# The first down product of a fused attention and two-MLP kernel: blocks of 512 tokens instead of 288

## The chip, the cores and the metric

The kernel runs on one core of one Trainium2 chip. The metric is the device time of one execution in microseconds. Beside it stands the profile of one execution, whose span runs from its first instruction to its last.

## The reference, cut to what matters

Two attentions follow each other (a packed query of 32 rows against 576 keys, then 576 queries against the 32 packed rows), and their output goes through two MLPs over 4608 tokens (8 batches of 576), with 512 features outside and 2048 inside:

```python
x = attention(q, attention(p, k, v))          # 4608 x 512
h = x @ w_in;   x = (h * np.cos(h)) @ w_out   # first MLP, d_ff 2048
h = x @ w_in2
g = np.where(h >= 1, h, np.where(h <= -1, 0.0, (h + 1) ** 2 / 4))
out = g @ w_out2                              # second MLP
```

## The kernel before, in words

All large products run on TensorE in float32r. For accuracy each operand is split into a high part and a remainder, and a product is three matmuls (`TERMS`: high times high, high times low, low times high) that add up in PSUM. Every matmul has a 128x128 stationary operand of its own and moves 288 columns (half a batch of 576 tokens).

The program has four stages, one after the other on TensorE.

- **up1** (L501 `up`): 128 items, each one half batch and one pair of 128-row tiles of d_ff. An item is 12 matmuls into `hps` and one ScalarE copy `u` (L516), which is stored to DRAM as `h1T` (late_store, L517). The attention's work is folded into the first items. The products that form an item's weights (`form`, L336) and the conversion of `w_out` (`cut_w_out`) lie among the items too. `hps` has two buffers, `u` five.
- **down1** (L720 `run_down1`): the product `g @ w_out` of the first MLP. It walks 16 blocks of 288 tokens. A block has 8 iterations, one for each pair of d_ff tiles, and an iteration is 24 matmuls (2 tiles of d_ff, 4 tiles of the output, 3 terms) at L745. So there are 128 iterations and 3072 matmuls. A block adds up in two PSUM tiles: tags X and Y in even blocks, two buffers of Z in odd ones; each tile is two PSUM banks of 512 float32 columns, of which `bank` (L582) hands out 288.
- **up2** (L790 `run_up2`) and **down2** (L909 `run_down2`): the second MLP, with seven products for eight of 2x2 blocks (X1, Z6, Y5 and so on). Its matmuls stand at L607 and L952.

An iteration i of down1 also makes ready what later iterations need. `load_h1(i + 7)` reads 288 tokens of `h1T`. `turn_k` (ScalarE, L691), `turn_t` (VectorE, L696), `turn_s` (ScalarE, a sine, L703) and `turn_m` (VectorE, L708) make h cos h; `part_hi` (ScalarE, L713) and `part_lo` (VectorE, L718) split it into `r`, which the matmuls move. All of these work on 128x576 elements. In the order written at L749 to L754 they run one to four iterations ahead of the matmuls that use them.

Further work in down1: `step("wt")` does one step of `combine` (L423), which converts the second MLP's weights into the forms of the seven products; a unit of weights is 13 steps, and down1 does 8 units, one in each 15 iterations. Each block's result is copied out of PSUM to `o` in the next block (ScalarE for c = 0, L761; VectorE for c = 1, L759) and stored as `yT`. `SU_AT` names the iterations that load converted weights (`load_su`), `Y_LOAD` and the last nine iterations prepare the first batch of up2 (`make_y`).

The order of instructions on each engine is the order in which they are written (`in_order`, L1198). All DMAs are issued from SP's queue, also in written order. A tile that takes over memory of a closed pool waits for the last user of that memory. The last seven items of up1 already carry the preparation of down1's first iterations (`begin`, L1194), and its first seven loads stand at every second of the last 14 items. Pools: `wpool` has eight buffers of 8 KB a partition, and `r`, `g` (the loads) and `t` have pools of their own (L1216 to L1218).

Of the kernel before, what the change touches and what calls it, by code (L numbers as in the profile page):

```python
# [23 lines left out]
SU_AT = tuple(range(70, 94, 4)) + (122, 124, 126, 127)  # L24
Y_LOAD = 112
# [12 lines left out]
def body(ctx: ExitStack, tc: tile.TileContext, q, k, v, p, w_in, w_out, w_in2, w_out2, out):  # L38
# [21 lines left out]
    dram = ctx.enter_context(tc.tile_pool(name="dram", bufs=1, space=bass.MemoryType.DRAM))  # L60

    yT = dram.tile([DM, NT], F32, name="yT")
    h1T = dram.tile([NFT // 2, 128, NT // HB, 2, HB], F32, name="h1T")
    su = dram.tile([2, 7, 128, 2, 2, 512], F32, name="su")
    sd = dram.tile([7, 2, 128, 4, 2, 256], F32, name="sd")
    gT = dram.tile([NFT // 2, 128, NT // HB, 2, HB], F32, name="gT")
# [22 lines left out]
    def late_store(dst, src):  # L89
        stores.append((dst, src))  # L90
# [410 lines left out]
    def up(n, hf, fp):  # L501

        c = fp // 2
        m, x = M[n, c], AT[n, hf]
        hps = ps_h.tile([128, 2, 512], F32, tag="h", name="hps")
        for j in range(2):
            cs = slice((fp % 2 * 2 + j) * 128, (fp % 2 * 2 + j) * 128 + 128)
            for G in range(2):
                for i, (w, y) in enumerate(TERMS):
                    nc.tensor.matmul(  # L510
                        out=hps[:, j, :HB], lhsT=m[:, w, G, cs], rhs=x[:, G, y],
                        start=(G == 0 and i == 0), stop=(G == 1 and i == 2),
                    )
        u = wk.tile([128, 2, HB], F32, tag="u", name="u", bufs=5)
        if True:
            last_act[:] = [nc.scalar.activation(out=u, in_=hps[:, :, :HB], func=AF.Copy).ins]  # L516
        late_store(h1T[fp, :, 2 * n + hf], u)  # L517


    KS = {"X1": 0, "Y5": 3, "X2": 1, "Z6": 4, "Y3": 6, "Z7": 5, "Z4": 2}  # L520
# [2 lines left out]
    n_s = [0]  # L523

    def s_tile(src):
        pool, tag, bufs = ((mpool, "m", 2), (wpool, "w", 8), (mpool, "o", 4))[(0, 0, 1, 1, 1, 1, 1, 1, 1, 1, 2, 2, 2, 2)[n_s[0] % 14]]
# [52 lines left out]
        tile_of("Z4", b21)  # L579
        yield  # L580

    def bank(x):  # L582
        return ps2.tile([128, 2, 512], F32, tag=x, name="ps" + x, bufs=2 if x == "Z" else 1)[:, :, :HB]

    def wtile(pool, tag, bufs):
        return pool.tile([128, 2, HB], F32, tag=tag, name=tag, bufs=bufs)
# [87 lines left out]

    pu, pd = ExitStack(), ExitStack()
    dn1 = {}

    G1 = {}

    def load_h1(i):  # L680
        if i < B * 16:
            t = dn1["g"].tile([128, 2, HB], F32, tag="g", name="h1")
            nc.sync.dma_start(out=t, in_=h1T[i % 8, :, i // 8])
            G1[i] = t

# [13 lines left out]

    def turn_s(i):  # L700
        if i < B * 16:
            t = turns[i]
            nc.scalar.activation(out=t, in_=t, func=AF.Sin, scale=2 * PI, bias=halfpi)  # L703

    def turn_m(i):
        if i < B * 16:
            t = turns[i]
            nc.vector.tensor_tensor(out=t, in0=G1.pop(i), in1=t, op=ALU.mult)  # L708

    def part_hi(i):  # L710
        if i < B * 16:
            r = parts[i] = dn1["r"].tile([128, 2, 2, HB], F32R, tag="r", name="r1")
            nc.scalar.activation(out=r[:, 0], in_=turns[i], func=AF.Copy)  # L713

    def part_lo(i):
        if i < B * 16:
            r = parts[i]
            nc.vector.tensor_tensor(out=r[:, 1], in0=turns.pop(i), in1=r[:, 0].bitcast(F32), op=ALU.subtract)  # L718

    def run_down1(w_out_ops):  # L720
        prep[:] = [ctx.enter_context(tc.tile_pool(name="prep", bufs=1, reuse_waits="tile"))]
        for x in range(5):
            up2[x] = ctx.enter_context(tc.tile_pool(name=f"up_{x}", bufs=1, reuse_waits="tile"))
        po = pd.enter_context(tc.tile_pool(name="dn_o", bufs=3, reuse_waits="tile"))
        streams["wt"].append(combine(units[N_FIRST:], prep_tiles))
        eng = [nc.vector]
        ys = make_y(0, eng)
        n_su = [0]
        order = [(ch, o) for ch in range(2) for o in ORDER_UP]

        for i in range(B * 16):
            blk, c = divmod(i, 8)
            if c == 0:
                acc = early if blk == 1 else [bank("Z") for _ in range(2)] if blk % 2 else [bank(x) for x in "XY"]
# [14 lines left out]
            part_lo(i + 1)  # L749
            turn_m(i + 2)  # L750
            turn_t(i + 3)
            turn_k(i + 4)
            part_hi(i + 2)
            turn_s(i + 3)  # L754
            begin_stores()
            if blk and c < 2:
                y = po.tile([128, 2, HB], F32, tag="o", name="o1")
                if c:
                    nc.vector.tensor_copy(out=y, in_=done[c])  # L759
                else:  # L760
                    nc.scalar.activation(out=y, in_=done[c], func=AF.Copy)  # L761
                late_store(
                    yT[c * 256:c * 256 + 256, (blk - 1) * HB:blk * HB].rearrange("(j p) t -> p j t", p=128), y
                )
# [4 lines left out]
            if i in SU_AT:  # L769
                load_su(*order[n_su[0]])  # L770
                n_su[0] += 1
            if i == Y_LOAD or i >= B * 16 - 9:
                next(ys)
        for c in range(2):
            y = po.tile([128, 2, HB], F32, tag="o", name="o1")
            if c:
                nc.vector.tensor_copy(out=y, in_=done[c])
            else:
                nc.scalar.activation(out=y, in_=done[c], func=AF.Copy)
            late_store(  # L780
                yT[c * 256:c * 256 + 256, NT - HB:].rearrange("(j p) t -> p j t", p=128), y
            )
# [7 lines left out]
    def run_up2():  # L790
# [7 lines left out]
        for p in range(B):  # L798
            for f in range(0, 8, 2):
# [10 lines left out]
                for k, o in enumerate(("X1", "Z4", "Z6", "Y5", "X2", "Z7", "Y3")):  # L810
# [375 lines left out]
    def item():  # L1186
        i = pos[0]
        for x in events[i]:
# [2 lines left out]
        begin_stores(1)  # L1191
        pos[0] += 1

    begin = [[lambda: turn_k(0), lambda: turn_t(0)], [lambda: turn_k(1), lambda: turn_t(1)],  # L1194
             [lambda: turn_s(0), lambda: turn_m(0)], [lambda: turn_k(2), lambda: turn_t(2)],
             [lambda: turn_s(1), lambda: turn_m(1), lambda: turn_k(3)],
             [lambda: part_hi(0), lambda: part_lo(0), lambda: turn_s(2), lambda: part_hi(1)], []]
    in_order = ordered(E.PE, E.Activation, E.DVE, E.SP, E.Pool)  # L1198
    if True:
        start()  # L1200
# [9 lines left out]
        while pos[0] < len(items):  # L1210
            i = pos[0]
            if i == len(items) - 16:
# [6 lines left out]
            if i >= len(items) - 14 and i % 2 == 0:  # L1219
                load_h1((i - len(items) + 14) // 2)  # L1220
            if i >= len(items) - 7:
                for x in begin[i - len(items) + 7]:
                    x()
# [59 lines left out]
```

## Time and profile before

| what | us |
|---|---|
| median of 3 runs (1474.38 to 1475.12) | 1474.67 |
| the profiled execution's own time | 1473.97 |
| its span, first to last instruction | 1472.2 |
| up1 in it, with the start | 0 to 339.1 |
| down1 | 339.1 to 748.7 |
| up2 | 748.7 to 1109 |
| down2 | 1109 to 1472 |

PE is TensorE, PEld its loading of stationary operands, DVE VectorE, ACT ScalarE, POOL GpSimd, SPq the queue from which SP issues DMAs. A line such as L745 is a line of the kernel before. Matmuls overlap in their pipeline: the mean of one (some 296 ns) is the time from its start to its last result, and the pace is read from how many fit into a stretch.

### The profile page before, as it was taken

How to read it: one execution, taken by the hardware profiler on the slowest of the kernel's cores; microseconds unless marked ns; L12 is line 12 of the kernel's file. 1: busy time of each engine (PE TensorE's matmuls, PEld its weight loads, DVE VectorE, ACT ScalarE, POOL GpSimd, SP SyncE). 2: the span in 40 equal slices, each digit the busy share in tenths (PEclk: the TensorE clock that was granted, in tenths of full speed). 3: DMA queues.
4: the chain of work that ended last, by engine and by line, in shares of the span. 5: the costliest groups of instructions: out<-in, count | busy, mean ns of one | idle time of the engine just before them, and what ended most of it. 6: DMA issues, size and time to landing. Idle time of an engine off the chain costs nothing.

```text
span 1472.2 us, 29608 instructions
## 1 busy us (share of the span) xinstructions
PE 1444.5 (98%) x11800; PEld 1390.2 (94%) x11800; DVE 1161.3 (79%) x1653; ACT 905.7 (62%) x1418; POOL 133.4 (9%) x85
## 2 busy tenths in 40 slices
PE   7999999999999999999999999999999999999998
PEld 5777878889999999999999999999999999999998
DVE  7875869778889888988846988889968777777775
ACT  4655666667767676766657777777775444444443
POOL 0000000000000000000005433533400000000000
PEclk9999999999999999999999999999999999999999
DMA  9777896675765567766664364664588544343350
GB/s 344 269 249 250 291 323 220 233 250 176 213 178 156 163 204 233 249 194 212 195 262 165 140 217 173 216 216 163 209 326 329 209 149 154 110 136 126 122 161 33
DMA packets 155961, 302.35 MB, mean 205 GB/s; under 512 B 13488, under 2 KB 59568, under 8 KB 152240
## 3 DMA queue, kind: packets, MB, share of 16 engines
q1 hardware_dynamic: 155824, 300.47, 60.2%
q8 instruction: 92, 1.51, 0.4%
q14 instruction: 45, 0.37, 0.1%
HBM read 176.69 MB, written 123.73 MB: 204 GB/s over the span
## 4 chain that ended last, share of the span: by engine, by line
PE 72%; DVE 2%; issue 1%; DMA 1%; ACT 0%; DVEq 0%; SPq 0%; ACTq 0%
PE psZ L745 14%; PE psZ L952 10%; PE psZ L607 9%; PE psY L745 7%; PE psX L745 7%; PE psX L952 7%; PE psY L952 6%; PE psY L607 6%; PE psX L607 6%; DMA t<-gT 1%; DVE t L627 1%; DVE hh L595 0%; PE hps L510 0%; DVE pa L147 0%; DVE u L595 0%
## 5 line engine op out<-in xcount | busy, mean ns | idle before, releaser
L510 PEld LDWEIGHTS hps<-at,m 128*128 128x128 f32 x1536 | 209.1, 191 | 41.6 <-ACT u L516 21.6
L510 PE MATMUL hps<-at,m 128*128 128x288 f32 x1536 | 222.9, 302 | 8.9 <-ACT u L516 5.5
L745 PE MATMUL psZ<-r,wo 128*128 128x288 f32 x1536 | 206.1, 296 | 0.0
L745 PEld LDWEIGHTS psZ<-r,wo 128*128 128x128 f32 x1536 | 205.2, 188 | 0.0
L855 ACT ACTIVATE r<-g 128x576 fp32r<-128x576 f32 x147 | 97.0, 681 | 123.3 <-DVE g L852 112.1
L77 POOL TENSOR_TENSOR ty<-yb,ty 128x576 fp32r<-128x576 f32 x51 | 85.6, 1678 | 935.0 <-ACT ty L76 934.2
L713 ACT ACTIVATE r<-t 128x576 fp32r<-128x576 f32 x128 | 87.6, 685 | 128.2 <-PE psY L745 61.3
L718 DVE TENSOR_TENSOR r<-t,r 128x576 fp32r<-128x576 f32 x128 | 96.9, 757 | 57.4 <-ACT r L713 57.1
L516 ACT ACTIVATE u<-hps 128x576 f32<-128x576 f32 x128 | 83.1, 649 | 79.5 <-PE hps L510 48.6
L745 PE MATMUL psY<-r,wo 128*128 128x288 f32 x768 | 123.1, 296 | 0.0
L745 PE MATMUL psX<-r,wo 128*128 128x288 f32 x768 | 123.1, 296 | 0.0
L627 DVE SCALAR_TENSOR_TENSOR t<-hh,t 128x576 f32<-128x576 f32 x128 | 122.2, 974 | 0.0
L619 ACT ACTIVATE t<-hh,half 128x576 f32<-128x576 f32 x128 | 98.9, 772 | 34.6 <-DVE hh L595 33.3
L865 DVE TENSOR_TENSOR r<-g,r 128x576 fp32r<-128x576 f32 x147 | 107.6, 753 | 4.7 <-ACT r L855 4.7
L745 PEld LDWEIGHTS psY<-r,wo 128*128 128x128 f32 x768 | 109.4, 188 | 0.0
L745 PEld LDWEIGHTS psX<-r,wo 128*128 128x128 f32 x768 | 109.3, 188 | 0.0
L952 PE MATMUL psZ<-r,so 128*128 128x288 f32 x768 | 104.8, 295 | 0.6 <-DVE hh L988 0.6
L952 PE MATMUL psY<-r,sw 128*128 128x288 f32 x768 | 104.6, 295 | 0.0
L952 PEld LDWEIGHTS psZ<-r,so 128*128 128x128 f32 x768 | 102.9, 188 | 0.8 <-DVE hh L988 0.8
L952 PEld LDWEIGHTS psY<-r,sw 128*128 128x128 f32 x768 | 102.8, 188 | 0.0
L708 DVE TENSOR_TENSOR t<-h,t 128x576 f32<-128x576 f32 x128 | 96.3, 752 | 1.8 <-ACT t L703 1.8
L696 DVE SCALAR_TENSOR_TENSOR t<-h,t 128x576 f32<-128x576 f32 x128 | 96.3, 752 | 1.8 <-ACT t L691 1.8
(170 smaller groups left out, 2625.0 us busy)
## 6 DMA issues: line engine op xcount, KB each, us to landing
h1T<-u SPq DMA_DIRECT2D x128, 288.0 KB, 4.2
h<-h1T SPq DMA_DIRECT2D x128, 288.0 KB, 3.9
gT<-t SPq DMA_DIRECT2D x128, 288.0 KB, 2.9
g<-gT SPq DMA_DIRECT2D x85, 288.0 KB, 3.7
raw<-in_moe_w_out SPq DMA_DIRECT2D x32, 512.0 KB, 6.7
t<-gT SPq DMA_DIRECT2D x36, 288.0 KB, 4.2
k<-in_k SPq DMA_DIRECT2D x8, 1152.0 KB, 9.1
yT<-o SPq DMA_DIRECT2D x32, 288.0 KB, 2.4
```

Source lines behind the costliest of these rows:

```text
L510: nc.tensor.matmul(out=hps[:, j, :HB], lhsT=m[:, w, G, cs], rhs=x[:, G, y], start=(G == 0 and i == 0), stop=(G == 1 and i == 2),)
L607: nc.tensor.matmul(out=ps[:, i], lhsT=s[:, d, w, cs], rhs=t[:, d, y], start=first and d == n == 0, stop=d == 1 and n == 2, skip_group_chec ...
L619: nc.scalar.activation(out=t, in_=st["h", o], func=AF.Relu, scale=0.5, bias=half)
L627: nc.vector.scalar_tensor_tensor(out=t, in0=st["h", o], scalar=1.0, in1=t, op0=ALU.max, op1=ALU.min)
L696: nc.vector.scalar_tensor_tensor(out=t, in0=G1[i], scalar=1 / (2 * PI), in1=t.bitcast(I32), op0=ALU.mult, op1=ALU.subtract)
L708: nc.vector.tensor_tensor(out=t, in0=G1.pop(i), in1=t, op=ALU.mult)
L713: nc.scalar.activation(out=r[:, 0], in_=turns[i], func=AF.Copy)
L718: nc.vector.tensor_tensor(out=r[:, 1], in0=turns.pop(i), in1=r[:, 0].bitcast(F32), op=ALU.subtract)
L745: nc.tensor.matmul(out=acc[d // 2][:, d % 2], lhsT=wo[f // 4, w][:, f % 4, ds], rhs=r[:, y, k], start=f == n == 0, stop=f == NFT - 1 and n ...
L855: nc.scalar.activation(out=r[:, 0], in_=b[out], func=AF.Copy)
L865: nc.vector.tensor_tensor(out=r[:, 1], in0=src, in1=r[:, 0].bitcast(F32), op=ALU.subtract)
L952: nc.tensor.matmul(out=ps[:, j], lhsT=w_[:, (2 * c + k) % 4, w, j * 128:j * 128 + 128], rhs=r[:, y, k], start=first_k and k == n == 0, sto ...
```

## The change

Down1 walks 9 blocks of 512 tokens, so 72 iterations of 24 matmuls with 512 columns each, and every instruction of the preparation covers 128x1024 elements. `h1T` is laid out with the tokens of all blocks side by side, so that a store writes 256 pieces of 288 floats and a load reads 256 pieces of 512. The three `r` tiles are taken from `wpool` and used in turn; the loads have 5 buffers in place of 7, `o` 2 in place of 3. A load stands 6 iterations ahead in place of 7. In an iteration the steps of the weights' conversion move ahead of `turn_t`; a unit's 13 steps now lie in 8 iterations (`STEPS_1`) and the eighth unit ends with iteration 63. The loads of converted weights and the first batch's preparation have new places (`SU_AT`, `Y_STEPS`), the preparation of down1's first iterations begins 12 items before the end of up1 in place of 7, and the first loads 16 items before in place of 14.

```diff
-    h1T = dram.tile([NFT // 2, 128, NT // HB, 2, HB], F32, name="h1T")
+    h1T = dram.tile([NFT // 2, 128, 2, NT], F32, name="h1T")
...
-        late_store(h1T[fp, :, 2 * n + hf], u)
+        t0 = n * S + hf * HB
+        late_store(h1T[fp, :, :, t0:t0 + HB], u)
...
-        pool, tag, bufs = (...)[(0, 0, 1, 1, 1, 1, 1, 1, 1, 1, 2, 2, 2, 2)[n_s[0] % 14]]
+        pool, tag, bufs = (...)[(0, 0, 1, 1, 1, 1, 1, 2, 2, 1, 1, 1, 2, 2)[n_s[0] % 14]]
...
-    def bank(x):
-        return ps2.tile([128, 2, 512], F32, tag=x, name="ps" + x, bufs=2 if x == "Z" else 1)[:, :, :HB]
+    def bank(x, n=HB):
+        return ps2.tile([128, 2, 512], F32, tag=x, name="ps" + x, bufs=2 if x == "Z" else 1)[:, :, :n]
...
+    TB = 512
+    N_DN = NT // TB * 8
...
-            t = dn1["g"].tile([128, 2, HB], F32, tag="g", name="h1")
-            nc.sync.dma_start(out=t, in_=h1T[i % 8, :, i // 8])
+            t = dn1["g"].tile([128, 2, TB], F32, tag="g", name="h1")
+            nc.sync.dma_start(out=t, in_=h1T[i % 8, :, :, i // 8 * TB:i // 8 * TB + TB])
...
-            r = parts[i] = dn1["r"].tile([128, 2, 2, HB], F32R, tag="r", name="r1")
+            r = parts[i] = dn1["r"][i % 3]
...
+    STEPS_1 = (1, 0, 3, 2, 1, 2, 2, 2)
+    SU_AT = (50, 53, 56, 66, 66, 68, 68, 70, 70)
+    Y_STEPS = {64: 1, 67: 2, 68: 2, 69: 2, 70: 2, 71: 1}
...
-        for i in range(B * 16):
+        for i in range(N_DN):
...
-            load_h1(i + 7)
+            load_h1(i + 6)
...
             part_lo(i + 1)
+            turn_k(i + 4)
             turn_m(i + 2)
+            part_hi(i + 2)
+            for _ in range(STEPS_1[i % 8] if i < 8 * UNITS_1 else 0):
+                step("wt")
             turn_t(i + 3)
-            turn_k(i + 4)
-            part_hi(i + 2)
             turn_s(i + 3)
             begin_stores()
             if blk and c < 2:
...
+                out_block(blk - 1, c, done[c])
...
-            if i < UNITS_1 * 15 and i % 15 not in (1, 2):
-                step("wt")
...
-    begin = [[lambda: turn_k(0), lambda: turn_t(0)], [lambda: turn_k(1), lambda: turn_t(1)],
-             [lambda: turn_s(0), lambda: turn_m(0)], [lambda: turn_k(2), lambda: turn_t(2)],
-             [lambda: turn_s(1), lambda: turn_m(1), lambda: turn_k(3)],
-             [lambda: part_hi(0), lambda: part_lo(0), lambda: turn_s(2), lambda: part_hi(1)], []]
+    begin = {12: ((turn_k, 0),), 11: ((turn_t, 0), (turn_k, 1)), 10: ((turn_t, 1), (turn_s, 0)),
+             9: ((turn_m, 0), (turn_s, 1)), 7: ((turn_m, 1), (turn_k, 2)), 6: ((turn_t, 2), (part_hi, 0)),
+             5: ((part_lo, 0), (turn_s, 2)), 3: ((part_hi, 1),), 2: ((turn_k, 3),)}
+    H1_AT = (16, 15, 14, 12, 10, 8)
...
-                dn1["g"] = pd.enter_context(tc.tile_pool(name="dn_g", bufs=7, reuse_waits="tile", side="right"))
-                dn1["r"] = pd.enter_context(tc.tile_pool(name="dn_r", bufs=3, reuse_waits="tile", side="right"))
+                dn1["g"] = pd.enter_context(tc.tile_pool(name="dn_g", bufs=5, reuse_waits="tile", side="right"))
+                dn1["r"] = [wpool.tile([128, 2, 2, TB], F32R, tag="w", name="r1") for _ in range(3)]
...
-    early = [bank("Z"), bank("Z")]
+    early = [bank("Z", TB), bank("Z", TB)]
```

`out_block(b, c, acc)` is the copy of a block's result from PSUM to `o` and its store to `yT`, as it stood in the loop before, with 512 tokens. With nine blocks the last one adds up in X and Y; with sixteen it was the two buffers of Z.

## Rows read from the trace of the kernel before

**Rows 1.** The page's first part (busy us of each engine) and its clock line.

```profile
PE 1444.5 (98%) x11800; PEld 1390.2 (94%) x11800; DVE 1161.3 (79%) x1653; ACT 905.7 (62%) x1418; POOL 133.4 (9%) x85
PEclk9999999999999999999999999999999999999999
```

**Rows 2.** Windows: length; busy us (instructions) of PE, PEld, DVE, ACT, POOL; clock; DMA.

```profile
316.90:339.10 22.20, 20.75 (x168) 19.52 (x161) 12.47 (x18) 17.09 (x27) 0.00 (x0) 1.00 0.74 254
339.10:748.70 409.60, 409.60 (x3074) 409.60 (x3073) 343.40 (x506) 276.44 (x439) 0.00 (x0) 1.00 0.62 196
748.70:760.00 11.30, 11.30 (x87) 11.30 (x86) 4.46 (x6) 5.44 (x9) 2.81 (x2) 1.00 0.92 342
```

**Rows 3.** Chain that ended last, first and last odd block: start, us, matmuls.

```profile
364.87 25.60 PE psZ L745 x192
...
723.27 25.60 PE psZ L745 x192
```

**Rows 4.** Who waited for the matmuls of L745 (us, times).

```profile
  ACT r L713: 118.3, 114
```

**Rows 5.** Windows, matmuls of L510, then of L1083: PE busy, PEld busy, clock, DMA.

```profile
34.42:39.22 4.80, 4.80 (x21) 4.80 (x21) 0.50 1.04 396
...
10.47:16.53 6.06, 6.06 (x26) 4.76 (x25) 1.00 1.03 353
```

**Rows 6.** Chain that ended last, in down2: start, us, matmuls.

```profile
1448.47 6.37 PE psZ L952 x48
```

**Rows 7.** Groups by form on DVE and ACT: busy, mean ns of one.

```profile
L708 DVE TENSOR_TENSOR t<-h,t 128x576 f32<-128x576 f32 x126 | 94.8, 752 | 0.0
L157 DVE TENSOR_TENSOR pa<-pa,raw 128x1024 f32<-128x1024 f32 x8 | 9.8, 1221 | 0.0
...
L145 DVE TENSOR_SCALAR pa<-raw 128x1024 int32<-128x1024 int32 x8 | 5.5, 686 | 0.0
...
L703 ACT ACTIVATE t<-t,halfpi 128x576 f32<-128x576 f32 x125 | 95.3, 763 | 0.0
L713 ACT ACTIVATE r<-t 128x576 fp32r<-128x576 f32 x126 | 86.3, 685 | 128.2 <-PE psY L745 61.3 <-PE psZ L745 56.9 <-DVE t L708 8.7
L138 ACT ACTIVATE raw<-raw 128x1024 f32<-128x1024 f32 x8 | 9.2, 1151 | 0.0
L342 ACT ACTIVATE m<-psM 128x1024 fp32r<-128x1024 f32 x3 | 3.1, 1024 | 0.0
```

**Rows 8.** Waits around down1: engine, line, waited for: us, times, longest.

```profile
DVE r L718 <- ACT r L713: 57.1, 84, 1.1
```

**Rows 9.** Timeline, last items of up1: start, us, instruction.

```profile
331.54 1.28 ACT L703 ACT_TABLE_LOAD   x1
...
333.52 0.63 ACT L516 ACTIVATE u<-hps 128x576 f32<-128x576 f32 x1
...
334.20 5.07 PE L510 MATMUL hps<-at,m 128*128 128x288 f32 x36 [1.45 <-ACT u L516]
```

**Rows 10.** Timeline, start of up2: start, us, instruction.

```profile
748.11 0.65 ACT L779 ACTIVATE o<-psZ 128x576 f32<-128x576 f32 x1 [4.94 <-PE psZ L745]
...
748.71 1.78 PE L607 MATMUL psX<-ty,sm 128*128 128x288 f32 x12
748.79 1.28 SPq L95 DMA_DIRECT2D yT<-o  x2
...
751.14 0.65 ACT L590 ACTIVATE p<-psX 128x576 f32<-128x576 f32 x1 [1.24 <-DMA yT<-o]
...
752.23 0.76 DVE L595 TENSOR_TENSOR u<-psZ,p 128x576 f32<-128x576 f32 x1 [2.56 <-DMA yT<-o]
```

**Rows 11.** DMA issues: KB each, median us to landing.

```profile
h1T<-u SPq DMA_DIRECT2D x128, 288.0 KB, 4.2
h<-h1T SPq DMA_DIRECT2D x128, 288.0 KB, 3.9
...
sd<-raw SPq DMA_DIRECT2D x24, 256.0 KB, 2.5
```

More of the change, by code (lines that the diff above doesn't have):

```diff
@@ L23 @@
 FIRST_AT = (29, 36, 37, 39, 42, 44, 45, 46, 52, 53, 55, 58, 60, 61, 68, 69, 71, 74, 76, 77, 78, 84, 85, 87, 90, 92)
-SU_AT = tuple(range(70, 94, 4)) + (122, 124, 126, 127)
-Y_LOAD = 112
 WO_SHARE = {4: 1.2, 9: 0.7, 10: 0.7, 12: 1.3, 13: 1.3, 14: 1.3, 15: 0.7}
@@ L525, in s_tile @@
     def s_tile(src):
-        pool, tag, bufs = ((mpool, "m", 2), (wpool, "w", 8), (mpool, "o", 4))[(0, 0, 1, 1, 1, 1, 1, 1, 1, 1, 2, 2, 2, 2)[n_s[0] % 14]]
+        pool, tag, bufs = ((mpool, "m", 2), (wpool, "w", 8), (mpool, "o", 4))[(0, 0, 1, 1, 1, 1, 1, 2, 2, 1, 1, 1, 2, 2)[n_s[0] % 14]]
         n_s[0] += 1
@@ L676, in body @@
     dn1 = {}
+    TB = 512
+    N_DN = NT // TB * 8
     G1 = {}
     def load_h1(i):
-        if i < B * 16:
-            t = dn1["g"].tile([128, 2, HB], F32, tag="g", name="h1")
-            nc.sync.dma_start(out=t, in_=h1T[i % 8, :, i // 8])
+        if i < N_DN:
+            t = dn1["g"].tile([128, 2, TB], F32, tag="g", name="h1")
+            nc.sync.dma_start(out=t, in_=h1T[i % 8, :, :, i // 8 * TB:i // 8 * TB + TB])
             G1[i] = t
@@ L688, in turn_k @@
     def turn_k(i):
-        if i < B * 16:
-            t = turns[i] = dn1["t"].tile([128, 2, HB], F32, tag="t", name="t")
+        if i < N_DN:
+            t = turns[i] = dn1["t"].tile([128, 2, TB], F32, tag="t", name="t")
             nc.scalar.activation(out=t.bitcast(I32), in_=G1[i], func=AF.Copy, scale=1 / (2 * PI), bias=0.25)
     def turn_t(i):
-        if i < B * 16:
+        if i < N_DN:
             t = turns[i]
@@ L700, in turn_s @@
     def turn_s(i):
-        if i < B * 16:
+        if i < N_DN:
             t = turns[i]
@@ L705, in turn_m @@
     def turn_m(i):
-        if i < B * 16:
+        if i < N_DN:
             t = turns[i]
@@ L710, in part_hi @@
     def part_hi(i):
-        if i < B * 16:
-            r = parts[i] = dn1["r"].tile([128, 2, 2, HB], F32R, tag="r", name="r1")
+        if i < N_DN:
+            r = parts[i] = dn1["r"][i % 3]
             nc.scalar.activation(out=r[:, 0], in_=turns[i], func=AF.Copy)
     def part_lo(i):
-        if i < B * 16:
+        if i < N_DN:
             r = parts[i]
             nc.vector.tensor_tensor(out=r[:, 1], in0=turns.pop(i), in1=r[:, 0].bitcast(F32), op=ALU.subtract)
+    STEPS_1 = (1, 0, 3, 2, 1, 2, 2, 2)
+    SU_AT = (50, 53, 56, 66, 66, 68, 68, 70, 70)
+    Y_STEPS = {64: 1, 67: 2, 68: 2, 69: 2, 70: 2, 71: 1}
     def run_down1(w_out_ops):
@@ L723, in run_down1, with out_block @@
             up2[x] = ctx.enter_context(tc.tile_pool(name=f"up_{x}", bufs=1, reuse_waits="tile"))
-        po = pd.enter_context(tc.tile_pool(name="dn_o", bufs=3, reuse_waits="tile"))
+        po = pd.enter_context(tc.tile_pool(name="dn_o", bufs=2, reuse_waits="tile"))
+        def out_block(b, c, acc):
+            y = po.tile([128, 2, TB], F32, tag="o", name="o1")
+            if c:
+                nc.vector.tensor_copy(out=y, in_=acc)
+            else:
+                nc.scalar.activation(out=y, in_=acc, func=AF.Copy)
+            late_store(yT[c * 256:c * 256 + 256, b * TB:b * TB + TB].rearrange("(j p) t -> p j t", p=128), y)
         streams["wt"].append(combine(units[N_FIRST:], prep_tiles))
@@ L729, in run_down1 @@
         order = [(ch, o) for ch in range(2) for o in ORDER_UP]
-        for i in range(B * 16):
+        for i in range(N_DN):
             blk, c = divmod(i, 8)
             if c == 0:
-                acc = early if blk == 1 else [bank("Z") for _ in range(2)] if blk % 2 else [bank(x) for x in "XY"]
-            load_h1(i + 7)
+                acc = early if blk == 1 else [bank("Z", TB) for _ in range(2)] if blk % 2 else [bank(x, TB) for x in "XY"]
+            load_h1(i + 6)
             r = parts.pop(i)
@@ L756, in run_down1 @@
             if blk and c < 2:
[L757 to L764, printed above, removed]
+                out_block(blk - 1, c, done[c])
             if c == 7:
                 done = acc
-            if i < UNITS_1 * 15 and i % 15 not in (1, 2):
-                step("wt")
-            if i in SU_AT:
+            while n_su[0] < len(SU_AT) and i == SU_AT[n_su[0]]:
                 load_su(*order[n_su[0]])
                 n_su[0] += 1
-            if i == Y_LOAD or i >= B * 16 - 9:
+            for _ in range(Y_STEPS.get(i, 0)):
                 next(ys)
         for c in range(2):
[L775 to L782, printed above, removed]
+            out_block(NT // TB - 1, c, done[c])
         begin_stores()
@@ L815, in run_up2 @@
                     if p == f == 0 and k < 4:
-                        if rest:
-                            load_su(*rest.pop(0)), load_su(*rest.pop(0))
+                        for _ in range(min(2, len(rest))):
+                            load_su(*rest.pop(0))
                         if k < 2:
@@ L1216, in body @@
                 dn1["t"] = pd.enter_context(tc.tile_pool(name="dn_t", bufs=4, reuse_waits="tile", side="right"))
-                dn1["g"] = pd.enter_context(tc.tile_pool(name="dn_g", bufs=7, reuse_waits="tile", side="right"))
-                dn1["r"] = pd.enter_context(tc.tile_pool(name="dn_r", bufs=3, reuse_waits="tile", side="right"))
[L1219 to L1223, printed above, removed]
+                dn1["g"] = pd.enter_context(tc.tile_pool(name="dn_g", bufs=5, reuse_waits="tile", side="right"))
+                dn1["r"] = [wpool.tile([128, 2, 2, TB], F32R, tag="w", name="r1") for _ in range(3)]
+            if len(items) - i in H1_AT:
+                load_h1(H1_AT.index(len(items) - i))
+            for x, j in begin.get(len(items) - i, ()):
+                x(j)
             item()
```

## The prediction, made before the changed kernel was run

> **What bounds the kernel now.** I read the page's busy shares first, then the windows by stage, the chain that ended last, and the waits of down1. TensorE is busy 98% of the span at the full clock [rows 1], and in down1 for all 409.6 us of 409.6, while VectorE is busy 84% and ScalarE 67% of it [rows 2]. The chain gives each odd block 25.60 us for its 192 matmuls, from the first to the last such block [rows 3]; the even ones between them fill the same time, since sixteen blocks of 25.60 us are 409.6 us. Others wait for the matmuls, among them ScalarE's `r` 114 times [rows 4]; TensorE itself waits for nobody in this stage. So down1 is worth 3072 matmuls times their pace, and the pace is 25.60 us / 192 = 133.33 ns for 288 columns. At 2.4 GHz, the level of the granted clock 1.00, 288 columns are 120 ns. What is over, 13.33 ns, is what the change can save: it moves the same columns (3072 x 288 = 1728 x 512) with fewer matmuls.
>
> **The pace at 512 columns** is the term that decides, and no row shows it. I have three neighbours. With the clock at 0.50 (1.2 GHz) the same kind of matmul in up1 starts every 240.0 ns (21 touch a window of 4.80 us, one of which started ahead of it) [rows 5]; 288 columns at 1.2 GHz are 240.0, so at half speed nothing is over. At full clock the keep-warm matmuls on plain float32 of 288 columns start every 6.06 us / 25 = 242.4 ns (26 touch the window, one of them early) [rows 5], which I take as two cycles a column, 240 ns, and 2.4 over. And in down2, where VectorE and ScalarE do less, the pace is 6.37 us / 48 = 132.7 ns [rows 6], so the 13 ns do not come from those engines. I conclude that something is over only where a column enters in each cycle of the 2.4 GHz clock. It can be a fixed sum per matmul: 133.33 ns are 320 cycles, 288 and 32, and a fixed time per matmul would vanish in the slower streams, as it does. It can be a loss per column, 320/288. Or it can be a floor of some 133 ns under the matmul which a longer stream would cover. I take the fixed sum, because 13.33 is a round 32 cycles and a loss of one column in nine has no such form, and because VectorE and ScalarE idling changed it little. Then one matmul takes 512 / 2.4 + 13.33 = 226.67 ns, and down1 takes 1728 x 226.67 = 391.7 us: **17.9 us less**. The bounds are a per-column loss, 133.33 x 512/288 = 237.0 ns and 409.6 us (nothing gained), and a floor that is covered, with 2.4 ns over as in the keep-warm row, 215.7 ns and 372.8 us (36.8 less).
>
> The Trainium skill (TensorE: Matmul & The Clock Gate, Back-to-back issue gap) gives the warm gap as the columns over 2.4 GHz and about 2.5 ns. By that rule 512 columns take 215.8 ns and the sum would be 36.7 us less in down1. The trace agrees at 242.4 ns for the keep-warm matmuls and disagrees at 133.33 ns for float32r, where the rule gives 122.5; so the measured pace decides, and I give the rule's outcome a small chance.
>
> **The preparation beside it.** An iteration becomes 24 x 226.67 = 5.44 us in place of 3.20. Of the preparation VectorE does three instructions in it. A 576-element one takes 752 ns, a 1024-element one 1221 [rows 7], so 72 x 3 x 1.221 = 263.7 us replace 128 x 3 x 0.752 = 288.8. VectorE's 343.4 us [rows 2] fall to some 318 to 331 (neighbours overlap a little, so not all of the 25 us show), 81 to 85% of 391.7: no tighter than before. ScalarE's three are 685, 763 and about 685 ns now; I put 1024 elements at 1.04 us, near the 1.024 of the copy of `m` and under the 1.151 of `raw` [rows 7], the sine at 1.14. That is 72 x 3.22 = 232 us for some 273. What sets the order is the exchange between the two engines: `turn_s`, `turn_m`, the steps of the weights and `turn_t` follow one another, 1.14 + 1.22 + steps + 1.22 us. The heaviest entries of `STEPS_1` are 0.69 + 1.22 = 1.91 us of VectorE [rows 7], which makes 5.49 us; the lightest, with no step, makes 3.58. `part_hi(i + 2)` may start only when matmuls i - 1 end, and its `part_lo` is wanted an iteration later; walking eight iterations, I find `part_lo` done 4 us or more before its matmuls. VectorE's 57.1 us of waits for `part_hi` [rows 8] show the same spare time now. I cost this at nothing; were the cover gone, the 5.49 us would cost 0.05 us in the two heaviest of eight iterations.
>
> **Moved DMAs.** A store of `h1T` is cut into 1152-byte pieces, where it had one of 2304 in each partition. Stores of 256 KB in 1 KB pieces land in 2.5 us, `h1T`'s in 4.2 [rows 11], so I cost that at nothing; the cover is the five `u` buffers. Loads of 512 KB for 288 have two iterations, 10.9 us, to land, against 3.9 us [rows 11] and an estimated 7. They stand on SP's queue behind the stores of `o` and the steps' own DMAs, whose waits cost load time but not that much. Moving `load_su` later puts four of its loads into iterations 66 to 68, 16 us or more before the first of them is used; the five that remain stand in up2's first three products, and are wanted two groups of seven products later.
>
> **The end of up1** carries nine ScalarE instructions ahead of down1, each some 0.36 us longer: 3.2 us more. ScalarE is busy 17.09 of the last 22.20 us there and TensorE 20.75 [rows 2], so it comes to about 20.3 and fills that stretch. Now TensorE stands 1.45 us, because the table load of 1.28 us and a sine come ahead of `u` [rows 9]. The new order spreads the nine over 11 items, four of them in items 116 to 119 together with the table load. In my walk of ScalarE's queue `u` is late by about a buffer in items 118 to 123, and down1 starts 0 to 1 us later; I take 0.5, with bounds of 1.45 less (the present stand goes) and 3.2 more (all of the extra shows).
>
> **The end of down1.** The last block now stands in X and Y, and up2 opens with X1. Its copy out of X (1.02 us) starts when the last of X's matmuls ends, and six matmuls of Y, 1.36 us, follow that: X is free in time, 0.1 us late at most. The copy's store to `yT` then covers the place of `p`: at present `p` starts 2.35 us after the store's issue [rows 10]; for 512 KB I allow 1 us more. X2 needs `p` 4.8 us after X1's start, so about 1 us is left; `u` has a like margin. I take 0.1, bounds 0 and 2.
>
> **Sum.** -17.9 + 0.5 + 0.1 = -17.3 us. The profiled execution takes 1473.97, its span 1472.2 and 1.8 around it, so 1456.7 would be its new time. The median is 0.7 above that execution: 1457.4.
>
> **Rivals.** (1) The rest is hidden: a floor, not a fixed sum. For it: the slower streams have next to nothing over. Against it: a load of stationary operands is under way in every case, and only the fast stream is slowed. 1474.67 - 36.8 + 0.6 = 1438.5. (2) The loss is per column, and the change does nothing for TensorE though the matmul count falls: 1474.67 + 0.6 = 1475.3. For it: it is absent wherever columns enter at half rate, as a limit on reading them would be. Against it: the round 32 cycles. (3) Slower: reads run ahead and cover the first columns, so that all of the 13.33 ns fall into the second half of the 288, which then takes 73.33 ns for 144 columns, 0.509 a column. The 224 columns more cost 114.1 ns, a matmul 247.4, and down1 427.5 us: 1474.67 + 17.9 + 0.6 = 1493.2. It decides from 0.467 ns for each further column on (a matmul of 237.9 ns). For it: half-rate streams lose nothing. Against it: no row shows a loss inside one matmul.
>
> **How the numbers follow.** A measurement of this kernel can tell about 0.2% (2.9 us) from no change. The fixed sum gets 0.62, the floor 0.08, the per-column loss 0.18, the slower case 0.12. Faster: 0.62 and 0.08, and a little of the per-column case (a part of the 13 ns fixed after all), 0.72; same 0.15; slower 0.13, by the slower case and by edges at their upper bounds. The range takes in the fixed sum with its edges (1455 to 1462), on the low side a pace half-way to the floor (221.2 ns, 382.2 us, 1448), on the high side the per-column loss with some of the edges' bounds (1477). It leaves out the floor and the slower case. I predict 1457.4.
>
> **What would show it.** Right: the windows of down1 show TensorE busy throughout over some 392 us, each block of 192 matmuls takes 43.5 us, and VectorE is busy 81 to 85%. Wrong at the pace: a block of 45.5 us (per column), 41.4 (floor) or 47.5. Wrong at the preparation: idle time ahead of the new matmul line, released by `part_lo`. Wrong at the edges: more than 1.45 us of stand for `u` in up1's last items, or a stand for `o` or `p` ahead of up2's X1 or X2.

## The result, and the profile of the changed kernel

The changed kernel takes 1457.91 us (median of 4 runs, 1454.81 to 1459.11) beside 1474.89 for the kernel before (4 runs, 1474.38 to 1476.88): a ratio of 0.9879, 95% interval 0.9861 to 0.9897. It is faster, as predicted; the forecast was 1457.4. The profiled execution took 1458.2 us, 0.3 over the median, with a span of 1456.4, 15.8 less than the span before.

Windows of the changed kernel, columns as in [rows 2]: about the last 16 items of up1 (a longer stretch than the 22.20 us there), down1, the start of up2, and a short stretch of up1 that comes up below.

```profile
311.00:342.07 31.07, 29.33 (x237) 25.69 (x236) 23.81 (x29) 24.66 (x34) 0.00 (x0) 1.00 0.83 287
342.07:733.70 391.63, 391.63 (x1729) 324.15 (x1729) 325.34 (x328) 251.94 (x263) 0.00 (x0) 1.00 0.61 198
733.70:745.00 11.30, 11.30 (x87) 11.30 (x86) 4.83 (x6) 5.13 (x9) 2.82 (x2) 1.00 0.94 355
211.07:214.48 3.41, 3.41 (x20) 3.04 (x13) 0.00 (x0) 1.60 (x3) 0.00 (x0) 0.50 1.08 376
```

Its chain that ended last, the first and the last odd block (start, us, matmuls).

```profile
385.59 43.52 PE psZ L759 x192
...
646.71 43.52 PE psZ L759 x192
```

Down1 went from 409.60 us [rows 2] to 391.6 with TensorE busy in all of it, and a block of 192 matmuls from 25.60 us [rows 3] to 43.52, which is 226.67 ns a matmul. VectorE is busy 325.34 / 391.63 = 83%, ScalarE 64%. One thing is new: stationary operands are being loaded (PEld) in 324.15 us of this stage, where it was all of it before.

The groups of the changed kernel that answer to [rows 7], from the page (busy us, mean ns of one, idle before it).

```profile
L704 ACT ACTIVATE t<-t,halfpi 128x1024 f32<-128x1024 f32 x72 | 82.9, 1151 | 70.8 <-DVE t L697 70.6
...
L714 ACT ACTIVATE r<-t 128x1024 fp32r<-128x1024 f32 x72 | 76.5, 1062 | 58.4 <-DVE t L709 26.5
...
L719 DVE TENSOR_TENSOR r<-t,r 128x1024 fp32r<-128x1024 f32 x72 | 87.9, 1220 | 9.3 <-ACT r L714 8.8
L709 DVE TENSOR_TENSOR t<-h,t 128x1024 f32<-128x1024 f32 x72 | 88.1, 1224 | 4.1
```

Waits of its down1, all engines (us in total, times, longest).

```profile
ACT t L704 <- DVE t L697: 70.6, 48, 3.2
DVE pa L143 <- ACT raw L136: 32.6, 8, 4.1
ACT r L714 <- DVE t L709: 26.5, 50, 4.0
ACT r L714 <- PE psY L759: 18.8, 11, 2.4
ACT r L714 <- PE psZ L759: 13.1, 8, 2.4
...
DVE r L719 <- ACT r L714: 7.6, 11, 2.8
```

No wait of the new matmul line (L759) is among them. ScalarE's `r`, which waited for the matmuls 114 times [rows 4], now does so 19 times; 98 times ScalarE waits for VectorE instead.

The rest of the span, stage by stage, worked out from the starts of the stages in both traces (item 112 is the 16th from the end of up1; an item starts with its matmuls):

| stage | before | after | difference |
|---|---|---|---|
| start to item 112 | 308.1 | 310.2 | +2.1 |
| item 112 to down1 | 31.0 | 31.7 | +0.7 |
| down1 | 409.6 | 391.7 | -17.9 |
| up2 | 359.7 | 358.3 | -1.4 |
| down2 to the end | 363.8 | 364.6 | +0.8 |

The place where up1 loses its 2.1 us, in the timelines of the kernel before and of the changed kernel. Item 66, ahead of it, starts 0.4 us earlier than before; item 69, behind it, 2.1 us later.

```profile
207.96 0.65 ACT L516 ACTIVATE u<-hps 128x576 f32<-128x576 f32 x1 [2.38 <-DMA h1T<-u]
...
209.20 0.72 PE L219 MATMUL psS<-k,pp 64*32 64x288 f32 x16 [1.37 <-ACT s L229]
```

```profile
208.53 0.65 ACT L514 ACTIVATE u<-hps 128x576 f32<-128x576 f32 x1 [3.40 <-DMA h1T<-u]
...
209.78 0.72 PE L217 MATMUL psS<-k,pp 64*32 64x288 f32 x16 [2.40 <-ACT s L227]
...
211.44 4.80 PE L508 MATMUL hps<-at,m 128*128 128x288 f32 x24
```

A `u` waits 3.40 us, 2.38 before, until an earlier store has left its buffer. TensorE stands 2.40 us, 1.37 before, runs some small matmuls, and then works at the granted clock 0.50 (1.2 GHz) for 3.41 us (fourth window row above), where the kernel before has 1.00. This fall of the clock doesn't come in every run: of the nine profiles of kernels with this up1 (the changed kernel twice and seven of the experiments), five show a clock of 0.91 over 205 to 225 us and reach item 112 at 310.2 to 313.8 us; four show 1.00 and reach it at 308.1 to 310.7.

In up2 the kernel before has one stand of TensorE of 1.6 us, for a sum on VectorE; the changed kernel has none.

```profile
PE psZ L607 <- DVE hh L595: 1.6, 1, 1.6
```

### The profile page after: what moved, and what is told of

Read it like the earlier page. It is cut to its first block, busy times and chain, and to the rows that moved or that the text cites. A ratio compares the mean times of both kernels' runs of the same rounds, so it can differ in the third digit from the quotient of the medians.

```text
span 1456.4 us, 26344 instructions
## 1 busy us (share of the span) xinstructions
PE 1429.6 (98%) x10456; PEld 1305.7 (90%) x10456; DVE 1147.2 (79%) x1478; ACT 884.2 (61%) x1243; POOL 134.2 (9%) x85
## 4 chain that ended last, share of the span: by engine, by line
PE 75%; DVE 1%; issue 1%; ACT 0%; DVEq 0%; ACTq 0%
PE psZ L759 12%; PE psZ L952 11%; PE psZ L606 10%; PE psX L759 7%; PE psY L759 7%; PE psX L952 7%; PE psY L952 7%; PE psY L606 6%; PE psX L606 6%; PE hps L508 0%; DVE t L626 0%; DVE hh L594 0%; DVE pa L145 0%; DVE u L594 0%; DVE pa L143 0%
## 5 line engine op out<-in xcount | busy, mean ns | idle before, releaser
L759 PE MATMUL psZ<-r,wo 128*128 128x512 f32 x768 | 174.7, 389 | 0.0
L759 PEld LDWEIGHTS psZ<-r,wo 128*128 128x128 f32 x768 | 144.1, 188 | 29.9
L704 ACT ACTIVATE t<-t,halfpi 128x1024 f32<-128x1024 f32 x72 | 82.9, 1151 | 70.8 <-DVE t L697 70.6
L759 PE MATMUL psX<-r,wo 128*128 128x512 f32 x480 | 121.8, 389 | 0.0
L759 PE MATMUL psY<-r,wo 128*128 128x512 f32 x480 | 121.8, 389 | 0.0
L759 PEld LDWEIGHTS psY<-r,wo 128*128 128x128 f32 x480 | 90.1, 188 | 18.7
L759 PEld LDWEIGHTS psX<-r,wo 128*128 128x128 f32 x480 | 90.0, 188 | 18.7
L719 DVE TENSOR_TENSOR r<-t,r 128x1024 fp32r<-128x1024 f32 x72 | 87.9, 1220 | 9.3 <-ACT r L714 8.8
L709 DVE TENSOR_TENSOR t<-h,t 128x1024 f32<-128x1024 f32 x72 | 88.1, 1224 | 4.1
L622 ACT ACTIVATE t<-t 128x576 f32<-128x576 f32 x128 | 87.8, 686 | 3.8
L697 DVE SCALAR_TENSOR_TENSOR t<-h,t 128x1024 f32<-128x1024 f32 x72 | 87.7, 1219 | 0.3 <-ACT t L692 0.3
L606 PE MATMUL psZ<-ty,sw 128*128 128x288 f32 x576 | 84.5, 296 | 0.0
L606 PE MATMUL psY<-ty,sw 128*128 128x288 f32 x576 | 84.5, 296 | 0.0
```

Of the source, the lines that this page charges most:

```text
L606: nc.tensor.matmul(out=ps[:, i], lhsT=s[:, d, w, cs], rhs=t[:, d, y], start=first and d == n == 0, stop=d == 1 and n == 2, skip_group_chec ...
L622: nc.scalar.activation(out=t, in_=t, func=AF.Square)
L697: nc.vector.scalar_tensor_tensor(out=t, in0=G1[i], scalar=1 / (2 * PI), in1=t.bitcast(I32), op0=ALU.mult, op1=ALU.subtract)
L759: nc.tensor.matmul(out=acc[d // 2][:, d % 2], lhsT=wo[f // 4, w][:, f % 4, ds], rhs=r[:, y, k], start=f == n == 0, stop=f == NFT - 1 and n ...
```

## The experiments

**The pace by itself.** Stretches of 384 matmuls, with nothing beside them (a first one, ahead of these, is left out here).

```python
stretch(mm_288, 288, 128, w, x, ...)      # L65: columns moved, stationary columns, float32r
stretch(mm_384, 384, 128, w, x, ...)      # L68
stretch(mm_512, 512, 128, w, x, ...)      # L71
stretch(mm_288_m64, 288, 64, w, x, ...)   # L74
stretch(mm_512_m64, 512, 64, w, x, ...)   # L77
stretch(mm_288_bf, 288, 128, wb, xb, ...) # L80: bf16
stretch(mm_512_bf, 512, 128, wb, xb, ...) # L83
```

> This kernel leaves out the whole computation: TensorE alone runs eight stretches of 384 matmuls each, ordered one after the other, every matmul with a stationary operand of its own. Theory (a fixed 32 cycles of 2.4 GHz per float32r matmul, 13.33 ns, whatever its columns): 288 columns 133.3 ns a matmul, 384 columns 173.3, 512 columns 226.7. Rival, a loss per column: 133.3, 177.8, 237.0. Rival, a floor under the short ones: 133.3, 162.4, 215.7. With a stationary operand of 64 columns in place of 128: if the 32 cycles come from loading it, 126.7 ns at 288 and 220.0 at 512; if they belong to the float32r matmul itself, still 133.3 and 226.7. With bfloat16 operands of 128 columns: if the sum belongs to 4-byte columns at the full clock, 122.5 and 215.8; if to any matmul, 133.3 and 226.7.

Groups of this kernel on TensorE, by form (busy us, mean ns of one).

```profile
L77 PE MATMUL p<-x,w 128*64 128x512 f32 x384 | 88.5, 392 | 0.0
L71 PE MATMUL p<-x,w 128*128 128x512 f32 x384 | 87.2, 389 | 0.0
L83 PE MATMUL p<-xb,wb 128*128 128x512 bf16 x384 | 83.0, 379 | 0.0
L68 PE MATMUL p<-x,w 128*128 128x384 f32 x384 | 66.7, 334 | 0.0
...
L65 PE MATMUL p<-x,w 128*128 128x288 f32 x384 | 50.7, 294 | 0.0
L74 PE MATMUL p<-x,w 128*64 128x288 f32 x384 | 50.1, 292 | 0.0
L80 PE MATMUL p<-xb,wb 128*128 128x288 bf16 x384 | 47.2, 286 | 0.0
```

Busy time less the last matmul's own time, over 383 intervals, is the pace; less the columns at 2.4 GHz it gives what is over:

| operand, columns | ns | over, ns |
|---|---|---|
| float32r, 288 | 131.6 | 11.6 |
| float32r, 384 | 173.3 | 13.3 |
| float32r, 512 | 226.7 | 13.3 |
| float32r, 288 and 512, 64 stationary columns | 130.0, 230.0 | 10.0, 16.7 |
| bf16, 288 and 512 | 122.5, 215.7 | 2.5, 2.4 |

What is over hardly grows from 288 columns to 384 and not from there to 512, so the per-column rival falls (237.0 ns at 512); it isn't covered by a longer stream, so the floor falls (215.7); and the slower case (247.4) falls. At 288 it is 1.7 ns less than the kernel's 13.33: by the starts of the matmuls in the trace, one interval in four is 127 ns and the others some 133. Why is open.

The loads of stationary operands beside the 288-column stretches (busy us, mean ns of one).

```profile
L65 PEld LDWEIGHTS p<-x,w 128*128 128x128 f32 x384 | 50.6, 188 | 0.0
L74 PEld LDWEIGHTS p<-x,w 128*64 128x64 f32 x384 | 49.9, 134 | 0.1
L80 PEld LDWEIGHTS <-wb 128*128 128x128 bf16 x384 | 37.5, 98 | 9.7 <-issue 0.3
```

With half as many stationary columns a load takes 134 ns in place of 188, while what is over falls by 1.6 ns at 288 columns and rises by 3.3 at 512; the rival that puts it down to the load had 6.7 ns at both. So it isn't the length of the load. It comes with float32r: bf16 pays 2.5 ns. Since the moving and the stationary operand changed their type together, it is not shown which of the two brings it. The Trainium skill (TensorE: Matmul & The Clock Gate, Back-to-back issue gap) gives the gap of a single matmul at the warm clock as the columns over 2.4 GHz and about 2.5 ns; the bf16 rows agree at 122.5 and 215.7 ns, the float32r rows don't.

**Blocks of 384 in the changed kernel**, a third size with all of the work around it (12 blocks, 96 iterations, the steps spread over 11 iterations):

```diff
-    TB = 512
+    TB = 384
...
-    STEPS_1 = (1, 0, 3, 2, 1, 2, 2, 2)
+    STEPS_1 = (1, 0, 2, 1, 2, 1, 1, 1, 2, 1, 1)
```

> The changed kernel in twelve blocks of 384 tokens, 2304 matmuls, the weights' units in 11 iterations each and the loads and first batch at the same distances from the end. Theory (13.33 ns a matmul over its columns): down1 2304 x 173.33 ns = 399.4 us, 7.7 more than in blocks of 512, the whole about 1465. Rival (the gain is not of the matmul's count but of the blocks' preparation and order): down1 at 391.7 or at 409.6.

It took 1466.09 us, a ratio of 0.9925 (0.9905 to 0.9945). Its down1 in the windows, columns as before.

```profile
338.58:737.95 399.37, 399.37 (x2306) 399.37 (x2305) 333.71 (x403) 265.95 (x338) 0.00 (x0) 1.00 0.61 197
```

2304 matmuls in 399.37 us are 173.34 ns each: 160.0 and 13.34. So the sum is the same at three sizes inside the kernel, 13.3 ns at 288, 384 and 512 columns.

**The layout of `h1T` alone**, in the kernel before. SP is busy longer with each store, 513 ns in place of 320 (medians of the issues between 40 and 310 us in the traces of the two kernels).

```diff
-    h1T = dram.tile([NFT // 2, 128, NT // HB, 2, HB], F32, name="h1T")
+    h1T = dram.tile([NFT // 2, 128, 2, NT], F32, name="h1T")
...
-        late_store(h1T[fp, :, 2 * n + hf], u)
+        late_store(h1T[fp, :, :, t0:t0 + HB], u)
...
-            nc.sync.dma_start(out=t, in_=h1T[i % 8, :, i // 8])
+            nc.sync.dma_start(out=t, in_=h1T[i % 8, :, :, i // 8 * HB:i // 8 * HB + HB])
```

> The kernel before with the new layout of h1T alone (stores in pieces of 1152 bytes, loads too), blocks of 288. My prediction's theory (the five u buffers hide it): within 1 us of the kernel before, ratio 1.000. Rival (the 2 us that the changed kernel's up1 lost ahead of its last items come from the store's longer issue, 513 ns for 320, which makes u wait for its buffer): 1.5 to 3 us slower, ratio 1.001 to 1.002, with the same 2 us in up1.

The median was 1475.98 us and the ratio 1.000 (0.9991 to 1.001), so the layout's own effect lies between 1.3 us less and 1.5 more. In its own profile the wait of `u` discussed above is 2.85 us, and down1 starts 1.7 us later than in the profile before; 1.2 of that is there ahead of this wait, 0.5 comes at it. In all ten profiles with the new layout the wait is 2.61 to 5.51 us, beside 2.38 in the one before. So the longer wait may have to do with the layout; what the interval excludes is that it costs 2 us in a typical run. And up1 doesn't lose them in every run: the kernel in blocks of 384, with the changed kernel's up1, reaches item 112 at 308.1 us, as the kernel before does.

**The order of the preparation**, put back as in the kernel before, steps last:

```diff
             part_lo(i + 1)
-            turn_k(i + 4)
             turn_m(i + 2)
-            part_hi(i + 2)
-            for _ in range(STEPS_1[i % 8] if i < 8 * UNITS_1 else 0):
-                step("wt")
             turn_t(i + 3)
+            turn_k(i + 4)
+            part_hi(i + 2)
             turn_s(i + 3)
...
+            for _ in range(STEPS_1[i % 8] if i < 8 * UNITS_1 else 0):
+                step("wt")
```

> The changed kernel, but inside an iteration the preparation stands in the order of the kernel before (turn_m, turn_t, turn_k, part_hi, turn_s, and the steps of the weights' conversion last). Theory (TensorE's pace alone sets down1, the preparation runs beside it with some 4 us to spare): down1 391.7 us, no idle time ahead of its matmuls, the whole within 2 us of the changed kernel. Rival (the new order is what lets VectorE keep up): TensorE waits for part_lo, down1 longer by 3 us or more.

1458.12 us, ratio 0.9877 (0.986 to 0.9894), and down1 took 391.71 us. The new order is not what the time came from.

**How much room VectorE has.** Two kernels make some `part_lo` write its result twice: 36 extra instructions of 1.22 us in the first (4 in each block), 18 in the second (2 in each). A third gives the first one other places for its steps.

```diff
-            nc.vector.tensor_tensor(out=r[:, 1], in0=turns.pop(i), ...)
+            t = turns.pop(i)
+            for _ in range(1 + i % 2):          # second kernel: 1 + (i % 4 == 1)
+                nc.vector.tensor_tensor(out=r[:, 1], in0=t, ...)
...
-    STEPS_1 = (1, 0, 3, 2, 1, 2, 2, 2)
+    STEPS_1 = (1, 1, 2, 2, 1, 2, 2, 2)         # third kernel alone
```

> The changed kernel with part_lo done twice in every second iteration: 36 more instructions of 1.22 us on VectorE, 4.9 us in each block of 43.5 us, where VectorE is busy for 37.7 now. Theory (cover of 4 us or more in each iteration): VectorE busy 42.5 of 43.5 us, TensorE still waits for nothing, down1 391.7 us to 393. Rival (ScalarE now waits for VectorE 70 us in down1, so VectorE has no slack left): down1 longer by 10 us or more, with idle time ahead of the matmuls until part_lo.

> The changed kernel with part_lo done twice in every fourth iteration: 18 more VectorE instructions of 1.22 us, 2.4 us in a block. With twice as many, down1 grew by 13.1 of 44 us, so some 31 us, 3.4 in a block, were still hidden. Theory (VectorE's room is a sum in each block: 43.5 us less 37.7 of work and about 3 of waits for ScalarE, some 2.9 us): down1 391.7 to 393 us, TensorE waits for nothing or nearly. Rival (every instruction added to VectorE's round with ScalarE is paid in part): about 6 us longer, 398.

> The kernel with 36 more VectorE instructions, but with the step that scales the raw weights on ScalarE moved from the third iteration of a unit to the second. There VectorE waited 2.2 us in each block for ScalarE, which did part_hi and then the scaling, while VectorE's next step was the conversion of what is scaled. Theory (VectorE's work of 42.7 us and its waits of 3.0 in a block set the pace of 45.8 us): without the 2.2 us a block is 43.5 us again, down1 392 to 395 us in place of 404.8. Rival (VectorE's work itself is too much, or the waits only move to another step): down1 still 402 us or more.

The first took 1471.75 us, a ratio of 0.9972 (0.9959 to 0.9985); its down1 grew by 13.1 us to 404.80, as its rival said. The second took 1455.67 in a single run beside 1475.98 for the kernel before, with down1 at 391.71, as its theory said. The third, in a single run too, took 1466.43 beside 1475.98, with down1 at 397.17: between the two theories' numbers.

Down1 of the first kernel: its window, its second and its fifth block, the waits of TensorE for `part_lo` (L721 there), and a wait inside a block.

```profile
346.10:750.90 404.80, 397.50 (x1730) 322.84 (x1729) 366.64 (x365) 251.19 (x263) 0.00 (x0) 1.00 0.59 192
389.64:433.16 43.52, 43.52 (x193) 36.07 (x192) 40.01 (x41) 27.34 (x29) 0.00 (x0) 1.00 0.55 167
523.76:569.51 45.75, 44.55 (x193) 35.83 (x192) 42.24 (x43) 28.87 (x31) 0.00 (x0) 1.00 0.58 179
```

```profile
PEld psZ L761 <- DVE r L721: 7.6, 9, 1.4
...
PE psZ L761 <- DVE r L721: 3.8, 6, 1.0
```

```profile
450.75 0.69 DVE L143 TENSOR_SCALAR pa<-raw 128x1024 int32<-128x1024 int32 x1 [2.18 <-ACT raw L136]
```

The first two blocks still take 43.5 us each. In them the lead of `part_lo`, from its end to the start of its matmuls, is used up: it is 3.1 us at the least in the first and 0.9 in the second, and from the third on TensorE waits. From the fourth to the eighth a block takes 45.7 to 45.8 us, so once the lead is gone the 4.9 us added cost 2.2. VectorE's work alone, 42.24 us in the fifth block, would fit into 43.5. But it also waits within the block, here 2.18 us for ScalarE's scaling of `raw`. The second kernel shows that 2.4 us more in a block cost nothing: its lead is 3.1 us at the least and doesn't shrink from block to block. So VectorE can take 2.4 us more per block of 43.5, but not 4.9; 4.9 less the 2.2 lost gives some 2.7, an estimate. In the third kernel the steps begin an iteration earlier, and the wait moves on.

Waits in the third kernel's down1.

```profile
ACT raw L136 <- DMA raw<-in_moe_w_in: 14.9, 6, 4.9
DVE t L709 <- ACT t L704: 10.7, 7, 4.6
```

ScalarE, now earlier at its scaling, waits for the load of `raw`, and VectorE for the sine behind it. That shows that the waits inside the block take part of the room; it doesn't show that they take all of it.

**The stand at the end of up1.** Timeline of the changed kernel there, beside [rows 9].

```profile
334.72 0.63 ACT L386 ACTIVATE wo<-w 128x512 fp32r<-128x512 f32 x1 [1.51 <-DVE w L155]
...
335.26 1.13 ACT L704 ACTIVATE t<-t,halfpi 128x1024 f32<-128x1024 f32 x1
...
336.30 1.17 ACT L514 ACTIVATE u<-hps 128x576 f32<-128x576 f32 x2
...
336.98 5.07 PE L508 MATMUL hps<-at,m 128*128 128x288 f32 x36 [1.62 <-ACT u L514]
```

TensorE waits 1.62 us for `u`, which stands behind a sine, which stands behind the conversion of `w_out`, which waits for VectorE. One kernel loads the sine's table earlier, another moves the third sine three items later, and its `turn_t` and the fourth `turn_k` by one.

```diff
+            if i == len(items) - 15:
+                nc.scalar.activation(out=tiny, in_=halfpi, func=AF.Sin)
```

> The changed kernel with one more ScalarE instruction, a sine of one element per partition 15 items before the end of up1, so that the table load of 1.28 us happens there. Theory (at the end of up1 ScalarE's queue is the limit and the 1.6 us for which TensorE waits for u come from the work ahead of that u): 0.5 to 1.3 us faster than the changed kernel, the wait for u in the last items under 0.6 us. Rival (the wait comes from the preparation's length alone, the table load being absorbed): within 0.3 us of the changed kernel, the wait still 1.6 us.

```diff
-             9: (...), 7: (...), 6: ((turn_t, 2), (part_hi, 0)),
-             5: ((part_lo, 0), (turn_s, 2)), 3: ((part_hi, 1),), 2: ((turn_k, 3),)}
+             9: (...), 7: (...), 6: ((part_hi, 0),),
+             5: ((turn_t, 2), (part_lo, 0)), 3: ((part_hi, 1),), 2: ((turn_s, 2),), 1: ((turn_k, 3),)}
```

> The changed kernel with turn_t(2), turn_s(2) and turn_k(3) moved one to three items later at the end of up1, so that neither VectorE's turn_t nor the sine stands ahead of the w_out step and of the two copies u that TensorE waits for. Theory (the wait of 1.6 us for u comes from ScalarE's idle 1.5 us for VectorE's conversion of w_out, behind turn_t(2), and from the sine of 1.15 us ahead of u): the longest wait for u in the last items falls under 0.6 us and the stretch from item 112 to down1's first matmul from 31.7 us to about 30.6, as long as before or shorter. Rival (ScalarE has simply too much to do there): the wait moves to another of the last items, and the stretch stays at 31.5 us or more.

The early table took 1455.47 us, a ratio of 0.9858 (0.9843 to 0.9873), but not for its reason. Its stretch from item 112 to down1 is 31.64 us, the changed kernel's 31.66: the stand halves and another comes up ahead of it. What made its total shorter is not shown.

```profile
317.59 1.86 PE L509 MATMUL hps<-at,m 128*128 128x288 f32 x12 [0.73 <-ACT u L515]
...
337.42 5.07 PE L509 MATMUL hps<-at,m 128*128 128x288 f32 x36 [0.78 <-ACT u L515]
```

The late sine does what it was to do: TensorE goes through the last 96 matmuls of up1 without a stand, and the stretch takes 29.78 us, 1.9 less than in the changed kernel and 1.2 less than before.

```profile
329.80 13.63 PE L508 MATMUL hps<-at,m 128*128 128x288 f32 x96
```

Its total, 1457.8 us, a ratio of 0.987 (0.9851 to 0.9889), can't be told from the changed kernel's: in this profile item 112 comes 3.3 us later than in the changed kernel's, and up to there the two programs are the same.

**The changed kernel again**:

> The changed kernel once more, beside the others on one chip, as what they are compared with. All theories: 0.988 of the kernel before, 1457 to 1459 us.

1460.3 us (1456.64 to 1462.6, 4 runs) beside 1475.87, a ratio of 0.9891 (0.9873 to 0.9908). Its down1 takes 391.71 us again; item 112 comes at 312.2 us, 2.0 later than in the first profile, and the stretch from there to down1 takes 33.25 us in place of 31.66, with two more short stands for `u`. So runs of one program differ by some microseconds ahead of down1 while down1 repeats to 0.1.

## Why the prediction was right

**The pace: right, to the digit.** The step took what is over at 288 columns, 13.33 ns, as a fixed sum; 226.67 ns and 391.7 us were predicted and measured. The 384-column kernel shows the same sum at a third size, the bare stretches with 128 stationary columns show it within 1.7 ns, and both exclude all three rivals. The arguments for it stand on less than it seemed. The slower streams differ in their type or their clock, and bf16 at full clock, with a column in each cycle, pays only 2.5 ns: of the cases run, only float32r at the full clock pays the large sum. And 13.33 ns is not always the round 32 cycles: the bare stretch at 288 has 11.6, and with 64 stationary columns it is 10.0 and 16.7. So the choice among the rivals, which got 0.62, was in part luck.

**The preparation at nothing: right.** TensorE waits for none of it, and VectorE's 325 us lie in the forecast 318 to 331. "`part_lo` done 4 us or more before its matmuls" came out as well: in the trace it ends 4.35 us or more ahead of them in all 72 iterations. One of the shortest leads, 446.34 to 450.70 us:

```profile
445.12 1.22 DVE L719 TENSOR_TENSOR r<-t,r 128x1024 fp32r<-128x1024 f32 x1
...
450.70 1.52 PE L759 MATMUL psX<-r,wo 128*128 128x512 f32 x6
```

What was wrong is how the lead was read afterwards, in the expectation of the first kernel with more work for VectorE: as room to be spent in each block. It is spent once, over the first two blocks. What VectorE can take on in every block is less, some 2.7 us by the estimate above, for part of its idle time goes to waits for ScalarE. ScalarE's terms were close: the sine 1.151 us for 1.14, `part_hi` 1.062 for 1.04.

**The moved DMAs at nothing: right within 1.5 us.** The reason given looked at the landing, and that held (4.4 us beside 4.2 [rows 11]; the 512 KB loads 5.1 for an estimated 7). The cost it didn't look at is SP's own time per store, 0.19 us longer; at 128 stores that is some 25 us of SP's queue. The total doesn't show it.

**The end of up1: right in the first profile.** +0.7 for +0.5; in the second profile of the changed kernel it is +2.3, inside the bounds. The stand for `u` stayed (1.62 us beside 1.45). The mechanism named is half of it: a sine stands ahead of `u`, but the table load doesn't, and ScalarE's wait of 1.51 us for VectorE's conversion of `w_out`, which comes ahead of both, is not in the prediction.

**The end of down1: right.** These rows of the changed kernel answer to [rows 10].

```profile
732.42 1.03 ACT L736 ACTIVATE o<-psX 128x1024 f32<-128x1024 f32 x1 [10.45 <-PE psX L759]
...
733.59 1.81 PE L606 MATMUL psX<-ty,sm 128*128 128x288 f32 x12
...
736.35 0.65 ACT L589 ACTIVATE p<-psX 128x576 f32<-128x576 f32 x1 [1.75 <-DMA yT<-o]
...
738.41 1.75 PE L606 MATMUL psX<-ty,sw 128*128 128x288 f32 x12
```

The copy ends 0.14 us before X1 starts, and `p` ends 1.4 us ahead of X2; about 1 us was expected. TensorE is busy all of the first 11.30 us of up2.

**What the sum didn't hold** is what lies outside its terms: +2.1 us in the earlier up1, -1.4 and +0.8 in up2 and down2. They add up to +1.5 us. The first varies by several microseconds between profiles of programs that are the same up to there (item 112 at 308.1 to 313.8 us), in part with the fall of the clock after the stand near 209 us, and up to 1.5 us of it may be the layout's. The second repeats and is a term that the sum lacked: up2 takes 359.7 and 359.8 us in the two profiles with blocks of 288, and 358.3 or less in the nine others. It is mostly the stand of 1.6 us that is gone; why it went was not tried. So the two profiled executions differ by 15.8 us, and the medians by 17.0 and, with the changed kernel run again, 15.6; that the forecast of 17.3 met the first median within 0.5 us is partly luck.

## What to carry to other kernels

Read the pace of a saturated TensorE as columns and a rest, and ask of the rest whether it is paid per matmul: with float32r at the full clock and 128 stationary columns it is 11.6 to 13.3 ns for each, so the same columns in fewer, wider matmuls save it (1344 fewer here, 17.9 us). The 5376 matmuls of up2 and down2 still move 288 columns; at 384 there would be 4032, and at 13.3 ns for each some 17.9 us less, an estimate that was not tried (down2 pays 12.7 now [rows 6], so it may be less). Before spending an engine's spare time, count its waits inside one period: how early one result is says only how long a shortfall stays hidden.

## What the runs showed that was not expected

- float32r and bf16 differ in what is over per matmul at the full clock, 13.3 ns and 2.5, though both take one column a cycle.
- With 64 stationary columns in place of 128 the 512-column matmul is no faster: 230.0 ns beside 226.7; at 288 it is 130.0 beside 131.6. Why it is 3.3 ns slower at 512 stays open.
- A kernel with too much work on VectorE (4.9 us more in each block) loses nothing in its first two blocks, which take 43.5 us like the changed kernel's, and 2.2 us in each once the lead is gone.
- A store of the same 288 KB keeps SP busy 513 ns as 256 pieces and 320 ns as 128, while it lands in 4.4 us beside 4.2.
